# The first block of an fp32 Strassen MLP computed by plain products in four PSUM banks, with its queue neighbours moved

## The chip, the cores and the metric

The kernel runs on one core of one Trainium2 chip. The metric is the device time of one execution in microseconds (us). Engines are named as the profile names them: PE is TensorE (its weight loads are PEld), DVE is VectorE, ACT is ScalarE, POOL is GpSimd, SP is SyncE, whose queue SPq issues the DMA transfers.

## The reference

A retention attention (8 batches, 8 heads, 576 positions, head size 64) is followed by an MLP over its 4608 tokens. Cut to what matters:

```python
scores = np.matmul(q, k.transpose(0, 1, 3, 2)) / np.sqrt(64)
ret = scores * Dmat                     # causal, gamma[h] ** (distance)
x = np.matmul(ret, v)                   # -> [4608 tokens, 512]
h = x @ w_in                            # [512, 2048]
g = h * erf(softplus(h))
return g @ w_out                        # [2048, 512]
```

The weights arrive in double precision, as pairs of 32-bit words, and the kernel rounds them to fp32 on the chip.

## The kernel before

The MLP's products dominate. They run in blocks: 9 chunks of 512 tokens times 4 column groups of w_in. The block (g, c) needs x[g, c] and the weights of group g. Both matrix multiplications use Strassen's scheme, seven products of half-sized operands instead of eight. A product is four matmuls, which the trace shows as eight records of 1.9 us together. Attention is cut into stages (transposes, scores, outputs of 128-token pieces), and `attend` places them between the products of group 0. While the first block runs, attention has only just produced the first chunk, and the first group's weights are still being rounded.

The sums of x for Strassen's scheme, and the store of a chunk for use by later groups:

```python
xpool = tc.tile_pool(name="xpool", bufs=2)      # chunk 2 reuses the buffer of chunk 0

def store_x(c):
    nc.sync.dma_start(out=xd[c], in_=x_stored.pop(c))

def operands_x(g, c):                            # b11..b22: the quarters of the tile
    ...
    if g == 0:
        tt(t1, b12, b11, ALU.subtract)
        tt(t2, b22, t1, ALU.subtract)
        tt(b12, b22, b12, ALU.subtract)          # in place: b12 is overwritten
        tt(t4, b21, t2, ALU.subtract)
        x_stored[c] = t
```

One part of the weights is rounded in five steps; `round_weights(n)` takes n steps further. A group has eight parts, four of w_in (parts 1 to 4 below) and four of w_out:

```python
nc.scalar.activation(a_f, high_f, AF.Abs)                 # L220, ScalarE
nc.scalar.mul(out=r_f, in_=low, mul=2.0**-52)             # L221
yield
nc.vector.tensor_scalar(...)                              # L225, VectorE
yield
nc.vector.tensor_scalar(...)                              # L229
yield
nc.vector.scalar_tensor_tensor(...)                       # L233
yield
nc.vector.tensor_scalar(...)                              # L238
nc.gpsimd.tensor_tensor(out=r_f, in0=high_f, in1=r_f, op=ALU.mult)   # L239, GpSimd
nc.gpsimd.tensor_tensor(out=a_f, in0=a_f, in1=r_f, op=ALU.add)       # L240
load_weights()          # DMA of a later part; needs a free buffer of four
yield
```

The last step also issues the load of a later part, in SyncE's queue.

The order in which the first block was issued:

```python
    round_weights(5); attend(done[0] + 2); round_weights(5)
    operands_x(0, 0)
    attend(done[0] + 3)
    ...
    steps = firsts[0].first()               # products A11, A12
    next(steps); round_weights(5); attend(done[0] + 3); round_weights(9)
    next(steps); attend(done[0] + 1)
    run(firsts[0].middle(), (0, 2, 3))      # products S2, S3, S1
    run(firsts[0].last(), (3, 3))           # products S4, A22, then softplus
    store_x(0)
    firsts[0].erf()
    most[0] = stages_for(3 * TCH) - 1
    while done[0] < stages_for(2 * TCH):
        attend(done[0] + 1); round_weights(4)
    operands_x(0, 1); store_x(1)
    run(firsts[1].first(), (3, 3))
    firsts[0].multiply()
```

Of the kernel before, what the change touches and what calls it, by code (L numbers as in the profile page):

```python
# [11 lines left out]
FP32 = mybir.dt.float32  # L12
# [6 lines left out]
P = 128  # L19
# [26 lines left out]
def kernel(  # L46
# [10 lines left out]
    nc = tc.nc  # L57
# [3 lines left out]
    TH = TCH // 2  # L61
# [4 lines left out]
    GP = 2  # L66
    GW = GP * P
    n_g = FH // GW
    W = GP * TH
# [9 lines left out]
    gpool = ctx.enter_context(tc.tile_pool(name="gpool", bufs=2))  # L79
    opool = ctx.enter_context(tc.tile_pool(name="opool", bufs=2))  # L80
    ps_at = ctx.enter_context(tc.tile_pool(name="ps_at", bufs=4, space=PSUM))
    ps_a = ctx.enter_context(tc.tile_pool(name="ps_a", bufs=2, space=PSUM))
    ps_e = ctx.enter_context(tc.tile_pool(name="ps_e", bufs=1, space=PSUM))
# [5 lines left out]
    def tt(out, in0, in1, op):  # L89
        nc.vector.tensor_tensor(out=out, in0=in0, in1=in1, op=op)  # L90
# [58 lines left out]
    A11, S3, A12, A22, S1, S2, S4 = range(7)  # L149
    B11, T3, B21, B22, T1, T2, T4 = range(7)  # L150
    weights = {}
# [96 lines left out]
    def round_weights(n=1):  # L248
        for _ in range(n):
            next(round_step, None)  # L250
# [13 lines left out]
    x = {}  # L264
# [117 lines left out]
    done = [0]  # L382

    def stages_for(tokens):

        last = max(i for i, (b, s0, _) in enumerate(pieces) if b * S + s0 < tokens)
        return stages.index((outputs, last)) + 1

    def attend(upto):
        while done[0] < min(upto, len(stages)):  # L390
            of, i = stages[done[0]]
            of(i)
            done[0] += 1
# [6 lines left out]
    def store_x(c):  # L400
        nc.sync.dma_start(out=xd[c], in_=x_stored.pop(c))
# [3 lines left out]
    def operands_x(g, c):  # L405
        t = x[g, c]
        b11, b12, b21, b22 = (t[:, 2 * d : 2 * d + 2, h * TH : (h + 1) * TH] for d in range(2) for h in range(2))
        t1, t2, t4 = (t[:, n_dc + j, :].rearrange("p (d i) -> p d i", d=2) for j in range(3))
# [3 lines that stand above are left out]
            tt(b12, b22, b12, ALU.subtract)  # L412
            tt(t4, b21, t2, ALU.subtract)
            x_stored[c] = t
        x[g, c] = {A11: b11, A12: b21, S4: b22, A22: t4, S1: t1, S2: t2, S3: b12}

    class First:
# [42 lines left out]
        def last(self):  # L460
            self.product(S4, self.a, False)
            nc.scalar.copy(out=self.t2[:, 0], in_=self.a)  # L462
            yield
            self.product(A22, self.e, False)
            tt(self.t1[:, 1], self.e, self.t1[:, 1], ALU.add)
            self.s = gpool.tile([P, 2, 2, W], FP32, tag="s", name="s")
            for j, t in enumerate((self.t1, self.t2)):
                nc.scalar.activation(self.s[:, j], t, AF.Softplus)  # L468
            yield

        def erf(self):
            for j in range(2):
# [100 lines left out]
    firsts = [First(g, c) for g, c in order]  # L573
# [22 lines left out]
    round_weights(5)  # L596
    attend(done[0] + 2)
    round_weights(5)
    operands_x(0, 0)
    attend(done[0] + 3)  # L600


    most = [stages_for(2 * TCH) - 1]

    def run(steps, rounds=(), stages=1):

        for step, _ in enumerate(steps):
            attend(min(done[0] + stages, most[0]))
            round_weights(rounds[step] if step < len(rounds) else 0)

    steps = firsts[0].first()
    next(steps)
    round_weights(5)
    attend(done[0] + 3)
    round_weights(9)
    next(steps)
    attend(done[0] + 1)
    run(firsts[0].middle(), (0, 2, 3))
    run(firsts[0].last(), (3, 3))
    store_x(0)  # L620
    firsts[0].erf()
    most[0] = stages_for(3 * TCH) - 1
    while done[0] < stages_for(2 * TCH):
        attend(done[0] + 1)
        round_weights(4)
    operands_x(0, 1)
    store_x(1)
    run(firsts[1].first(), (3, 3))
    firsts[0].multiply()
    for b, nxt in zip(blocks[1:], blocks[2:] + [None]):  # L630
        n = order.index((b.g, b.c))
# [10 lines left out]
        elif n + 2 < n_s:  # L642
            f = firsts[n + 1]
# [53 lines left out]
```

## Time and profile before

| | before |
|---|---|
| time, median of 3 runs | 1086.6 us (1084.09 to 1086.61) |
| span of the profiled run | 1083.4 us, mean granted PE clock 0.99 |
| PE busy | 1053.2 us |
| PE idle between 37 and 103.4 us | 19.5 us |
| PE idle after 104 us | 2.1 us, then the end |

### The profile page before, as it was taken

To read this page: it belongs to the slowest core of one execution; us is meant where nothing else is said; L and a number is where in the kernel's file an instruction comes from. 1 tells how busy PE (TensorE), PEld (TensorE's weight loads), DVE (VectorE), ACT (ScalarE), POOL (GpSimd) and SP (SyncE) were. 2 spreads that over 40 slices of the span, in tenths; PEclk is the share of its full clock that TensorE was granted. 3 is DMA by queue.
4 is the path that set the end of the run, shared out by engine and by line. 5 is a ranking of instruction groups with operands and counts; after the bars stand their busy time and mean duration, and the time that the engine had idled before them with its cause. 6 is when DMAs were issued, how large, how long until landed. Compare 5 with 4: busy or idle time off the path is not lost.

```text
span 1083.4 us, 15779 instructions
## 1 busy us (share of the span) xinstructions
PE 1053.2 (97%) x6514; PEld 904.8 (84%) x6514; DVE 611.5 (56%) x942; ACT 395.2 (36%) x494; POOL 143.6 (13%) x142
## 2 busy tenths in 40 slices
PE   9596999999999999999999999999999999999997
PEld 7475888888888888888888888888888888888886
DVE  3856766576567664455565545565555444544544
ACT  2243323413414244433334444333344433333341
POOL 2523222131212300001001100100011000000000
PEclk9898999999999999999999999999999999999999
DMA  9968668686594252355555534545443333444432
GB/s 184 224 146 252 146 185 227 138 236 156 153 225 133 77 194 107 146 185 197 200 204 206 183 147 146 185 184 200 187 194 147 146 146 146 149 183 186 192 135 77
DMA packets 186488, 185.65 MB, mean 171 GB/s; under 512 B 148017, under 2 KB 160817, under 8 KB 178353
## 3 DMA queue, kind: packets, MB, share of 16 engines
q1 hardware_dynamic: 186272, 184.31, 54.5%
q8 instruction: 51, 0.84, 0.3%
q10 hardware_dynamic: 144, 0.33, 0.1%
q14 instruction: 21, 0.16, 0.0%
HBM read 130.36 MB, written 61.34 MB: 177 GB/s over the span
## 4 chain that ended last, share of the span: by engine, by line
PE 93%; DVE 3%; DMA 1%; POOL 1%; issue 1%; ACT 1%; SPq 0%; POOLq 0%; DVEq 0%
PE a L506 23%; PE a L426 23%; PE g L506 12%; PE g L426 11%; PE e L426 6%; PE e L506 6%; PE s L308 3%; PE o L320 3%; PE o L331 3%; PE kv L343 2%; PE pt_k L298 1%; DMA xd<-x 1%; PE idle L585 1%; DVE x L90 0%; DVE sT L90 0%
## 5 line engine op out<-in xcount | busy, mean ns | idle before, releaser
L426 PE MATMUL a<-x,wa 128*128 128x256 f32 x1152 | 277.7, 384 | 10.1 <-DVE x L90 6.1
L426 PEld LDWEIGHTS a<-x,wa 128*128 128x128 f32 x1152 | 217.8, 191 | 41.2 <-issue 6.3
L506 PE MATMUL a<-wb,s 128*128 128x256 f32 x864 | 205.8, 381 | 2.1 <-DVE o L90 2.1
L506 PEld LDWEIGHTS a<-wb,s 128*128 128x128 f32 x864 | 162.5, 190 | 25.9 <-DVE o L90 2.4
L90 DVE TENSOR_TENSOR t<-g,t 128x512 f32<-128x512 f32 x72 | 49.8, 692 | 163.2 <-ACT t L456 120.7
L426 PE MATMUL g<-x,wa 128*128 128x256 f32 x576 | 137.2, 381 | 0.0
L90 DVE TENSOR_TENSOR o<-a,o 128x512 f32<-128x512 f32 x108 | 74.3, 688 | 105.3 <-PE a L506 104.2
L426 PEld LDWEIGHTS g<-x,wa 128*128 128x128 f32 x576 | 108.2, 190 | 14.8
L239 POOL TENSOR_TENSOR wraw<-wraw 128x512 f32<-128x512 f32 x32 | 33.9, 1058 | 491.5 <-DVE wraw L238 195.3
L451 ACT COPY t<-a 128x512 f32<-128x512 f32 x36 | 21.1, 586 | 193.0 <-PE a L426 193.0
L90 DVE TENSOR_TENSOR t<-t,s 128x1024 f32<-128x1024 f32 x72 | 86.5, 1242 | 0.0
L468 ACT ACTIVATE s<-t 128x1024 f32<-128x1024 f32 x72 | 72.1, 1048 | 29.6 <-DVE t L90 29.6
L426 PE MATMUL e<-x,wa 128*128 128x256 f32 x288 | 71.8, 393 | 6.3 <-POOL wa L240 6.3
L462 ACT COPY t<-a 128x512 f32<-128x512 f32 x36 | 21.1, 586 | 146.7 <-PE a L426 146.7
L473 ACT ACTIVATE s<-s 128x1024 f32<-128x1024 f32 x72 | 72.1, 1049 | 0.4
L506 PE MATMUL g<-wb,t 128*128 128x256 f32 x288 | 68.6, 381 | 0.0
L506 PE MATMUL a<-wb,t 128*128 128x256 f32 x288 | 68.5, 381 | 0.0
L506 PE MATMUL e<-wb,t 128*128 128x256 f32 x288 | 68.5, 381 | 0.0
L506 PE MATMUL g<-wb,s 128*128 128x256 f32 x288 | 68.5, 380 | 0.0
L426 PEld LDWEIGHTS e<-x,wa 128*128 128x128 f32 x288 | 55.6, 196 | 14.9 <-POOL wa L240 6.9
L456 ACT COPY t<-a 128x512 f32<-128x512 f32 x36 | 21.1, 585 | 113.4 <-PE a L426 113.4
L90 DVE TENSOR_TENSOR sT<-s,cst 128x512 f32<-128x512 f32 (+1 forms) x80 | 47.0, 629 | 26.8 <-PE s L308 26.7
(64 smaller groups left out, 1243.1 us busy)
## 6 DMA issues: line engine op xcount, KB each, us to landing
x<-xd SPq DMA_DIRECT2D x27, 1792.0 KB, 10.7
od<-o SPq DMA_DIRECT2D x54, 512.0 KB, 3.8
o<-od SPq DMA_DIRECT2D x27, 1024.0 KB, 6.9
xd<-x SPq DMA_DIRECT2D x9, 1792.0 KB, 7.0
out_dram<-o SPq DMA_DIRECT2D x17, 512.0 KB, 2.8
raw_k<-in_k_dram SPq DMA_DIRECT2D x64, 128.0 KB, 4.7
raw_v<-in_v_dram SPq DMA_DIRECT2D x64, 128.0 KB, 3.8
wraw<-in_moe_w_in_dram SPq DMA_DIRECT2D x32, 256.0 KB, 4.7
```

The lines of the kernel that those rows point to most:

```text
L90: nc.vector.tensor_tensor(out=out, in0=in0, in1=in1, op=op)
L239: nc.gpsimd.tensor_tensor(out=r_f, in0=high_f, in1=r_f, op=ALU.mult)
L308: nc.tensor.matmul(ps[e][:n, p, :n], lhsT=t["kT"][r, p, :n], rhs=t["qT"][r, p, :n], start=True, stop=True)
L320: nc.tensor.matmul(o[e * D : (e + 1) * D, p, :n], lhsT=t["v"][:n, 2 * p + e, :], rhs=t["sT"][:n, e, p, :n], start=(p == 0), stop=(s0 == 0 ...
L331: nc.tensor.matmul(o[r, p, :n], lhsT=kept["state"][r, p, :], rhs=t["qT"][r, p, :n], start=False, stop=(p == NP - 1), skip_group_check=True,)
L343: nc.tensor.matmul(kv[e * D : (e + 1) * D, p, :], lhsT=t["k"][:n, 2 * p + e, :], rhs=t["v"][:n, 2 * p + e, :], start=(p == 0), stop=(p == ...
L426: nc.tensor.matmul(acc[:, j * TH : (j + 1) * TH], lhsT=weights["wa", self.g][:, a, d, j * P : (j + 1) * P], rhs=x[self.g, self.c][a][:, d, :],
L451: nc.scalar.copy(out=self.t1[:, 1], in_=self.a)
L456: nc.scalar.copy(out=self.t2[:, 1], in_=self.a)
L468: nc.scalar.activation(self.s[:, j], t, AF.Softplus)
L473: nc.scalar.activation(self.s[:, j], self.s[:, j], AF.Erf)
L506: nc.tensor.matmul(acc[:, tp, :], lhsT=left[:, j * TH + tp * P : j * TH + (tp + 1) * P], rhs=weights["wb", self.g][:, b, j, :], start=(sta ...
```

## The change

The intent is to let TensorE begin while weights are still being rounded. Strassen's second product, A12, already needs parts 3 and 4, and later ones need sums of x and sums of weights. Eight plain products need neither: the first four use only parts 1 and 2, and the last four add parts 3 and 4 in the same four PSUM banks. The four sums of x, which stood in VectorE's queue just before the block, move behind it, and the store of the chunk with them. Softplus and erf of the block, and the rounding of parts 3 and 4, take other places in their queues.

```diff
+        def plain(self):
+            acc = [ps_a.tile([P, W], FP32, tag="a", name=f"p{n}") for n in range(2)]
+            acc += [ps_e.tile([P, W], FP32, tag=n, name="p" + n) for n in "eg"]
             ...
+            for half, slots in enumerate(((A11, S3), (A12, A22))):
+                for n in range(4):
+                    tok, f = n // 2, n % 2
+                    for j in range(GP):
+                        for d in range(2):
+                            nc.tensor.matmul(acc[n][:, j * TH : (j + 1) * TH],
+                                lhsT=wa[:, slots[f], d, j * P : (j + 1) * P],
+                                rhs=t[:, 2 * half + d, tok * TH : (tok + 1) * TH], ...)
+                    if half == 1:
+                        nc.scalar.copy(out=(self.t2 if tok else self.t1)[:, f], in_=acc[n])
+                    yield
             ...
     round_weights(5)
-    operands_x(0, 0)
     attend(done[0] + 3)
+    round_weights(5)
             ...
-    steps = firsts[0].first()
-    next(steps)
-    round_weights(5)
-    attend(done[0] + 3)
-    round_weights(9)
-    next(steps)
-    attend(done[0] + 1)
-    run(firsts[0].middle(), (0, 2, 3))
-    run(firsts[0].last(), (3, 3))
+    for step, _ in enumerate(firsts[0].plain()):
+        attend(min(done[0] + 1, most[0]))
+        round_weights((0, 5, 0, 0, 2, 2, 2, 2)[step])
+    operands_x(0, 0)
     store_x(0)
-    firsts[0].erf()
+    round_weights(2)
     most[0] = stages_for(3 * TCH) - 1
     while done[0] < stages_for(2 * TCH):
         attend(done[0] + 1)
-        round_weights(4)
+        round_weights(3)
+    firsts[0].softplus()
     operands_x(0, 1)
     store_x(1)
-    run(firsts[1].first(), (3, 3))
+    for _ in firsts[1].first():
+        attend(done[0] + 1)
+        round_weights(3)
+    firsts[0].erf()
     firsts[0].multiply()
```

(Cuts are marked with dots; the matmul's arguments are joined to fewer lines. The lines that make softplus a method of its own are left out.)

More of the change, by code (lines that the diff above doesn't have):

```diff
@@ L465, in last, with softplus @@
             tt(self.t1[:, 1], self.e, self.t1[:, 1], ALU.add)
+            self.softplus()
+            yield
+        def plain(self):
+            acc = [ps_a.tile([P, W], FP32, tag="a", name=f"p{n}") for n in range(2)]
+            acc += [ps_e.tile([P, W], FP32, tag=n, name="p" + n) for n in "eg"]
+            self.t1, self.t2 = (gpool.tile([P, 2, W], FP32, tag=f"t{n}", name=f"t{n}") for n in (1, 2))
+            wa, t = weights["wa", self.g], x[self.g, self.c]
+            for half, slots in enumerate(((A11, S3), (A12, A22))):
[3 more added lines that the diff above has]
+                        for d in range(2):
+                            nc.tensor.matmul(
+                                acc[n][:, j * TH : (j + 1) * TH],
+                                lhsT=wa[:, slots[f], d, j * P : (j + 1) * P],
+                                rhs=t[:, 2 * half + d, tok * TH : (tok + 1) * TH],
+                                start=(half == j == d == 0),
+                                stop=(half == d == 1),
+                                skip_group_check=True,
+                            )
+                    if half == 1:
+                        nc.scalar.copy(out=(self.t2 if tok else self.t1)[:, f], in_=acc[n])
+                    yield
+        def softplus(self):
             self.s = gpool.tile([P, 2, 2, W], FP32, tag="s", name="s")
@@ L468, in last @@
                 nc.scalar.activation(self.s[:, j], t, AF.Softplus)
-            yield
         def erf(self):
```

## The prediction

> **What bounds the kernel now.** I read first the page's busy line, then its slices, then TensorE's list of waits in the first 200 us, then TensorE's instructions in order of time, then the other queues around each gap.
>
> ```profile
> PE 1053.2 (97%) x6514; PEld 904.8 (84%) x6514; DVE 611.5 (56%) x942; ACT 395.2 (36%) x494; POOL 143.6 (13%) x142
> ...
> PE   9596999999999999999999999999999999999997
> ...
> PEclk9898999999999999999999999999999999999999
> ```
>
> TensorE (PE) is the bound: 30 us of a span of 1083.4 us are not busy, and the only low slices are in the first 110 us (one slice is 27 us) and the last. From 104 us on, the waits list shows TensorE waiting 2.1 us in all, near the end. So a microsecond gained on TensorE before 104 us is gained at the end; nothing else is. The waits list of the first 200 us names the large ones (total, times, longest):
>
> ```profile
> PE e L426 <- POOL wa L240: 6.3, 2, 4.5
> PE a L426 <- DVE x L90: 6.1, 1, 6.1
> PE a L426 <- POOL wa L240: 4.0, 1, 4.0
> ```
>
> Line 426 is a Strassen product of the first matrix multiplication, L240 the last step of rounding one part of its weights. TensorE in order of time (start, length, instruction, count, idle before):
>
> ```profile
> 40.99 2.60 PE L426 MATMUL a<-x,wa 128*128 128x256 f32 x6 [3.97 <-POOL wa L240]
> ...
> 49.49 0.70 PE L426 MATMUL e<-x,wa 128*128 128x256 f32 x2 [1.80 <-POOL wa L240]
> 54.67 2.93 PE L426 MATMUL e<-x,wa 128*128 128x256 f32 x6 [4.48 <-POOL wa L240]
> ...
> 84.77 0.68 PE L308 MATMUL s<-qT,kT 64*64 64x64 f32 x16 [2.13 <-ACT kT L299]
> 85.39 3.47 PE L426 MATMUL e<-x,wa 128*128 128x256 f32 x8
> ...
> 95.58 3.75 PE L426 MATMUL a<-x,wa 128*128 128x256 f32 x8 [6.08 <-DVE x L90]
> ```
>
> With the small ones (0.29, 0.17, 0.62), idle time from 37 to 103.4 us is 19.5 us. A second loss is visible: eight records take 3.47 or 3.75 us after a gap, but 1.9 elsewhere. One-microsecond windows show a granted clock of 0.50 at 41.3-44.7, 51.6-58.4, 85.7-89.1 and 92.5-99.3 us. Busy time in them, times the missing clock, is about 1.7 + 1.9 + 1.7 + 1.9 = 7.2 us. So 26.7 us can be won here, 2.5% of the time, if every wait vanished.
>
> The 6.08 us at 95.58 end a longer story, seen in the queues of VectorE (DVE) and of DMA issue (SPq):
>
> ```profile
> 75.77 6.98 SPq L203 DMA_DIRECT2D wraw<-in_moe_w_in_dram  x4
> 82.80 0.59 SPq L401 DMA_DIRECT2D xd<-x  x1
> ```
>
> ```profile
> 92.17 0.42 DVE L90 TENSOR_TENSOR x<-o,cst 128x256 f32<-128x256 f32 x1 [8.01 <-DMA xd<-x]
> ```
>
> The store of the first chunk of x stands behind weight loads that wait for a raw buffer; it is issued at 82.8 and lands 9.3 us later; only then may VectorE write chunk 2 into that buffer, and only then come the sums of chunk 1, for which TensorE waits.
>
> **What the Trainium skill says.** "TensorE: Matmul & The Clock Gate", Part 1: the array's clock is halved after an idle window of about 3.4 us and restored after a busy one, and the window runs freely. The trace agrees: the half-clock stretches begin and end on a grid of 3.41 us (41.3, 44.7, 51.6, 58.4, 85.7, 89.1), and a gap of 2.13 us was enough where it left the window 62% idle. "SBUF — State Buffer", Who interferes with whom: a VectorE instruction with two SBUF inputs, or in a two-port mode, and a GpSimd instruction exclude each other; one with a single SBUF input does not. It agrees: the sums of x at 37.68 us took 5.26 us for four beside GpSimd, 2.61 at 94.03 without it, and L239 1.36 us instead of 1.04; the score masks, read from PSUM, took 1.28 for two either way.
>
> **The change, part by part.** Seven Strassen products of block 0 become eight plain ones: +1 product, 8 records, +1.9 us of TensorE. The four sums of x leave the VectorE queue at 37.7 us and come after the block; four combining additions (0.69 us each) vanish, off the path. A plain product of the first half needs only weight parts 1 and 2, so four of them, with the attention stages between, now cover the rounding of parts 3 and 4. I followed the built order of all queues by hand, with durations from this trace (product 1.9, outputs 2.66 with states, scores 1.09, a pair of transposes 0.88, an L225-L229-L233-L238 chain 0.46+0.45+0.70+0.43, L239+L240 2.4).
>
> Gap 1. Part 2 ends its VectorE chain at 37.77 as before. GpSimd no longer meets the x sums, so L239+L240 take 2.4 instead of 3.0: ready at 40.35, not 40.94. Idle 3.4 us, half clock again.
>
> Gap 2, at parts 3 and 4, closes. TensorE: first product to 44.0, transposes 45.1, product 47.0, attention outputs 48.65 (its kv matmuls release the VectorE queue), product 50.55, scores 51.65, product 53.55, transposes 54.45. Part 4: VectorE 48.65 + state and x 1.0 + chain 2.1 = 51.75, GpSimd to 54.25. The fifth product needs it at 54.8: no wait, with half a microsecond to spare. Before, this gap cost 1.80 + 4.48 and 1.9 of clock.
>
> The rest of the plain block runs to 66.7 and the next outputs to 69.35. **Here a new wait appears:** in VectorE's queue, between those outputs and the score mask of the next stage, now stand the tail of a rounding (0.45 + 0.70), all four sums of chunk 0 (2.6) and L238 (0.43). Mask ready at 69.35 + 1.05 + 4.2 + 0.6 = 75.2; TensorE has only scores and a short transpose pair left, to 71.0. Idle 4.2 us, then a half-clock window, -1.7. This does not depend on absolute times: about 5.8 us of VectorE against 1.65 of TensorE.
>
> The store follows the sums at 74.2-74.8 instead of 82.8 and now stands ahead of the blocked weight load. With its median of 7.0 us (5.7 to 9.3) it lands near 81.5; VectorE reaches the write at 80.7. Then the rounding tail, slowed by GpSimd, and two of chunk 1's sums end at about 86. TensorE, at half clock from 75.2 to 78.6, has done outputs, the first two products of block 1, scores and transposes by 84.8: idle 1.2 instead of 6.08, and a warm clock. The 2.13 us for kT at 84.77 vanishes: the erf calls and their table load no longer stand before that copy. After that I find 0.4 us for the next mask, and 1.5 for another (VectorE has a weight sum and a multiply before it): the outputs that started at 108.61 now start near 98.2 and end near 99.9 against 109.63.
>
> The sum: idle 3.4 + 4.2 + 1.2 + 0.4 + 1.5 = 10.7 us against 19.5; clock 3.4 against 7.2; one more product, 1.9. Saved 8.8 + 3.8 - 1.9 = 10.7 by this sum, 9.7 by the running times. Three rounding steps of the output weights move into the loop, where TensorE has no waits. I take 10 off the 1086.6 us median: 1076.5.
>
> **The rivals.** (a) VectorE becomes the early bound. For: gap 2's margin is 0.5 us and the mask wait is mine from the order alone; if GpSimd and VectorE exclude each other more than I counted, the fifth product waits 1-2 us and another half-clock window falls: gain 4-6, time 1081-1083. (b) The store still decides. For: it took 9.3 us once, under load; the DMA share in 30-50 us is above 1. Then the third product of block 1 waits 3-4 us and goes cold: 1080. Against: fewer loads are issued beside it now. (c) The change does what its author hoped, and the mask wait is short because VectorE got the sums done early: they depend on no TensorE wait except the block's end. Against: they stand behind the outputs in a strict queue. Then 5-6 us more: 1070. (d) The extra product merely replaces idle time and nothing moves: 1086. Against: waits of 10 us are cut by dependence, not by chance.
>
> **Range and chances.** The errors of some six waits, each about a microsecond, and of one or two clock windows of 1.7 us give 3-4 us; the runs of before spread by 2.5 us. 8 in 10: 1071 to 1082. Faster by over 2% needs 1064.9, 21.7 us of the 26.7: 2 in 100. Slower by over 2% would need a new loss of 30 us in a stretch of 70: 1 in 100.
>
> **What would show it.** Right: TensorE's list has no GpSimd wait above 1 us except one of 3-3.5 us near 40 us; one of about 4 us for a score mask near 71-75; the chunk-0 store issued near 74-75; two half-clock stretches instead of four. After 104 us no new waits. Wrong: a GpSimd wait near 54 us (step gap 2), a VectorE wait on the store above 3 us, no mask wait near 75, or a steady stretch after 110 us that is not the same length as before.

## More of the kernel before

PE is busy for 97% of the span, and the whole loss that can be won lies in the first tenth. The view of stretches shows where. Its columns are: the stretch, its length, then the busy time of PE, PEld, DVE, ACT and POOL with the number of instructions, the granted PE clock, the DMA share and GB/s. Two of its lines for the kernel before:

```profile
50.00:60.00 10.00, 5.52 (x21) 4.55 (x21) 6.04 (x8) 1.08 (x2) 3.94 (x4) 0.66 0.89 177
...
90.00:100.00 10.00, 4.42 (x25) 3.19 (x25) 5.96 (x12) 1.81 (x4) 1.72 (x2) 0.66 0.83 247
```

In each of these stretches of ten microseconds PE has work for about half, and the mean clock granted over the stretch is 0.66. No other engine is full in them (the DMA share is 0.89 and 0.83), so they look like waits on an order of things rather than on throughput.

## The result, and the profile after

| | before | after |
|---|---|---|
| time, median | 1085.86 us (4 runs, 1084.09 to 1086.61) | 1075.51 us (4 runs, 1075.12 to 1076.22) |
| ratio | | 0.9908, 95% interval 0.9891 to 0.9925 |
| span of the profiled run | 1083.4 us | 1074.0 us |
| PE idle in the stretch of the first two blocks | 19.5 us | 9.4 us (2.01 + 4.16 + 1.10 + 0.67 + 1.30 + 0.15) |

A ratio here is the mean time of one kernel's runs over the mean of the other's runs of the same rounds, so it is not quite the ratio of the medians. The change is 0.9% faster. The predicted 1076.5 us is 1 us off.

The page of the changed kernel, its slices of PE and of PE's clock (40 slices of 27 us):

```profile
PE   8888999999999999999999999999999999999997
...
PEclk9889999999999999999999999999999999999999
```

The deep slice that "before" had (a 5 in the second place) is gone, but the first four slices are still not full, and the clock is still below its full value in two of them.

The stretches of the changed kernel, with the columns explained above:

```profile
50.00:60.00 10.00, 10.00 (x97) 8.26 (x96) 4.02 (x8) 1.66 (x3) 3.96 (x4) 1.00 0.98 170
...
70.00:80.00 10.00, 5.84 (x57) 4.70 (x54) 8.29 (x15) 5.12 (x7) 4.22 (x5) 0.66 0.80 256
...
90.00:100.00 10.00, 8.55 (x63) 6.92 (x64) 9.97 (x13) 2.79 (x5) 6.63 (x4) 1.00 1.07 321
```

The hole at 50-60 us is closed, the one at 90-100 us nearly so, and a new one stands at 70-80 us. TensorE's largest waits in the first 200 us (line, what was waited for, total, times, longest):

```profile
PE o L320 <- ACT s L495: 4.2, 1, 4.2
PE o L320 <- DVE sT L90: 2.8, 5, 1.0
PE p L480 <- POOL wa L240: 2.0, 1, 2.0
...
PE a L426 <- DVE x L90: 1.1, 1, 1.1
```

Against the list of before, the GpSimd waits fell from 10.3 us to 2.0, the wait for the sums of x from 6.1 to 1.1, and a wait of 4.2 us in an attention output (L320) came in. TensorE in order of time in the changed kernel (start, length, instruction, count, idle before):

```profile
40.22 2.93 PE L480 MATMUL p<-x,wa 128*128 128x256 f32 x6 [2.01 <-POOL wa L240]
...
54.11 1.89 PE L480 MATMUL p<-x,wa 128*128 128x256 f32 x8
...
74.68 2.52 PE L320 MATMUL o<-sT,raw_v 128*64 128x128 f32 x16 [4.16 <-ACT s L495]
...
85.97 1.96 PE L426 MATMUL a<-x,wa 128*128 128x256 f32 x8 [1.10 <-DVE x L90]
...
98.82 0.40 PE L320 MATMUL o<-sT,raw_v 128*64 128x128 f32 x2 [1.30 <-issue]
...
100.85 1.99 PE L532 MATMUL e<-wb,t 128*128 128x256 f32 x8
```

The product at 54.11 is the fifth, the first that needs parts 3 and 4; it starts with no wait at all. The last line is the second product of the second matrix multiplication. In the kernel before, the same product stands here in TensorE's order of time:

```profile
110.22 1.99 PE L506 MATMUL e<-wb,t 128*128 128x256 f32 x8
```

So by this product the change is 110.22 - 100.85 = 9.37 us ahead. The spans differ by 1083.4 - 1074.0 = 9.4 us. All that was won was won before 101 us, and nothing was lost later. From there on, the list of either kernel has the same wait, of 2.1 us in total for an output tile.

What ended the new wait at 74.68 is seen in VectorE's order of time:

```profile
71.03 2.61 DVE L90 TENSOR_TENSOR x<-x 128x512 f32<-128x512 f32 x4
73.56 0.42 DVE L238 TENSOR_SCALAR wraw<-wb 128x512 uint32<-128x512 uint32 x1
73.90 1.28 DVE L90 TENSOR_TENSOR sT<-s,cst 128x512 f32<-128x512 f32 x2
...
80.09 0.42 DVE L90 TENSOR_TENSOR sums<-kv,state 128x256 f32<-128x256 f32 x1 [1.63 <-PE kv L343]
80.43 0.75 DVE L90 TENSOR_TENSOR x<-o,cst 128x256 f32<-128x256 f32 x2
...
83.70 4.42 DVE L90 TENSOR_TENSOR x<-x 128x512 f32<-128x512 f32 x4
```

The mask of the next scores (sT, third line) stands behind the four sums of chunk 0 (first line) and a rounding step. Its first instruction ends near 73.90 + 0.68 = 74.58, and TensorE goes on at 74.68. The waits list names a ScalarE activation as the releaser instead, one that ended at about 74.47. In two of the experiments below (sums behind the mask, sums deferred) the same matmul again follows its mask by 0.10 or 0.11 us while the list names another ScalarE instruction. And where the softplus is put elsewhere (experiment "activations back") the list names VectorE. So the mask is the releaser, and the name in the list is that of whichever other instruction finished about then.

The two lines of SyncE's queue that answer the held-up store of before:

```profile
73.67 0.34 SPq L401 DMA_DIRECT2D xd<-x  x1
76.68 1.67 SPq L203 DMA_DIRECT2D wraw<-in_moe_w_in_dram  x2
```

The store of chunk 0 is issued at 73.67 instead of 82.80, and now ahead of the weight loads. VectorE writes into the freed buffer at about 80.8 (the line at 80.43 above, its second instruction) with no wait, where before it had waited 8.01 us.

### The profile page after: what moved, and what is told of

It reads as the page before. It is cut to its first block, busy times and chain, and to the rows that moved or that the text cites. A ratio compares the mean times of both kernels' runs of the same rounds, so it can differ in the third digit from the quotient of the medians.

```text
span 1074.0 us, 15808 instructions
## 1 busy us (share of the span) xinstructions
PE 1053.1 (98%) x6522; PEld 905.2 (84%) x6522; DVE 610.3 (57%) x939; ACT 395.7 (37%) x494; POOL 146.3 (14%) x142
## 4 chain that ended last, share of the span: by engine, by line
PE 93%; DVE 3%; SPq 2%; issue 1%; DMA 1%; ACT 0%; POOL 0%; DVEq 0%; ACTq 0%
PE a L532 23%; PE a L426 22%; PE g L532 12%; PE g L426 11%; PE e L532 6%; PE e L426 6%; PE o L320 3%; PE s L308 3%; PE o L331 3%; SPq L131 2%; PE kv L343 2%; PE pt_k L298 1%; PE p L480 1%; DMA raw_v<-in_v_dram 1%; DVE x L90 1%
## 5 line engine op out<-in xcount | busy, mean ns | idle before, releaser
L426 PE MATMUL a<-x,wa 128*128 128x256 f32 x1120 | 266.8, 381 | 1.1 <-DVE x L90 1.1
L426 PEld LDWEIGHTS a<-x,wa 128*128 128x128 f32 x1120 | 210.5, 190 | 30.4 <-ACT kT L299 1.3
L90 DVE TENSOR_TENSOR o<-a,o 128x512 f32<-128x512 f32 x108 | 74.2, 687 | 105.6 <-PE a L532 104.2
L426 PE MATMUL g<-x,wa 128*128 128x256 f32 x560 | 133.2, 381 | 0.0
L426 PEld LDWEIGHTS g<-x,wa 128*128 128x128 f32 x560 | 105.3, 190 | 14.4
L451 ACT COPY t<-a 128x512 f32<-128x512 f32 x35 | 20.5, 586 | 184.9 <-PE a L426 184.9
L462 ACT COPY t<-a 128x512 f32<-128x512 f32 x35 | 20.5, 586 | 148.5 <-PE a L426 148.5
L426 PE MATMUL e<-x,wa 128*128 128x256 f32 x280 | 66.7, 381 | 0.0
L532 PEld LDWEIGHTS g<-wb,t 128*128 128x128 f32 x288 | 54.2, 190 | 7.6
L532 PEld LDWEIGHTS g<-wb,s 128*128 128x128 f32 x288 | 54.2, 190 | 7.5
## 6 DMA issues: line engine op xcount, KB each, us to landing
x<-xd SPq DMA_DIRECT2D x27, 1792.0 KB, 10.7
```

Of the source, the lines that this page charges most:

```text
L90: nc.vector.tensor_tensor(out=out, in0=in0, in1=in1, op=op)
L426: nc.tensor.matmul(acc[:, j * TH : (j + 1) * TH], lhsT=weights["wa", self.g][:, a, d, j * P : (j + 1) * P], rhs=x[self.g, self.c][a][:, d, :],
L451: nc.scalar.copy(out=self.t1[:, 1], in_=self.a)
L532: nc.tensor.matmul(acc[:, tp, :], lhsT=left[:, j * TH + tp * P : j * TH + (tp + 1) * P], rhs=weights["wb", self.g][:, b, j, :], start=(sta ...
```

## The experiments

All were timed in five rounds against the kernel before, each on the same chip as the runs of before that stand beside it, on three different chips. All outputs are right. The changed kernel was not run again beside them, so an experiment is set against it by the two ratios to before: a difference of 0.001 is 1.1 us. An interval is about 0.0015 wide to either side (0.0017 for the changed kernel), so differences under about 2.5 us, the two errors taken together, are not taken as shown by the times alone.

| run | edit of | median us (runs) | before us | ratio (95%) |
|---|---|---|---|---|
| changed kernel | | 1075.51 (4) | 1085.86 | 0.9908 (0.9891 to 0.9925) |
| sums behind the mask | changed | 1078.99 (5) | 1085.22 | 0.9943 (0.9930 to 0.9956) |
| sums deferred | changed | 1073.88 (4) | 1085.22 | 0.9898 (0.9883 to 0.9913) |
| store early | before | 1081.38 (5) | 1085.22 | 0.9964 (0.9952 to 0.9977) |
| activations back | changed | 1074.94 (4) | 1085.22 | 0.9908 (0.9895 to 0.9922) |
| third part late | changed | 1076.96 (6) | 1086.03 | 0.9914 (0.9899 to 0.9928) |
| part one first | changed | 1073.49 (4) | 1086.03 | 0.9878 (0.9862 to 0.9895) |
| deferred and part one first | changed | 1070.82 (4) | 1086.03 | 0.9856 (0.9840 to 0.9871) |
| store late | changed | 1080.26 (6) | 1086.03 | 0.9946 (0.9932 to 0.9960) |
| rounding in the gaps | changed | 1079.03 (5) | 1086.10 | 0.9943 (0.9929 to 0.9957) |
| all three | changed | 1068.76 (4) | 1086.10 | 0.9839 (0.9825 to 0.9852) |
| all three, store first | changed | 1063.99 (6) | 1085.44 | 0.9805 (0.9791 to 0.9819) |

My theory after the result: about 10 us of idle time are gone because the rounding gap at parts 3 and 4 closed and because the store left earlier; about 4 us came back as the mask wait. The rivals: the store's place is incidental; or the activations' move did part of it; or the mask wait is all that keeps the change from winning more.

### Store early, in the old kernel

This does one part of the change alone: in the kernel before, the store moves ahead of the block's middle. Its data has been ready since the sums.

```diff
     attend(done[0] + 1)
+    store_x(0)
     run(firsts[0].middle(), (0, 2, 3))
     run(firsts[0].last(), (3, 3))
-    store_x(0)
```

> The kernel before, with only the store of chunk 0 moved ahead of the blocked weight loads (Strassen's first block kept). My theory: the 8 us wait of VectorE for that store is gone, the third product of block 1 starts near 89.5-90.5 instead of 95.6, then a new wait of about 2 us for the transposed q eats some: 4 to 7 us faster than before, 1079 to 1082. So more than half of the gain is the store's place. Rival (the gain is the plain block's closing of the rounding gaps): under 2 us faster.

Measured: ratio 0.9964, 3.8 us faster than before, just under the expected range. SyncE's issue and TensorE's third product of block 1 in this run:

```profile
67.49 0.89 SPq L401 DMA_DIRECT2D xd<-x  x1
```

```profile
91.80 3.47 PE L426 MATMUL a<-x,wa 128*128 128x256 f32 x8 [2.61 <-DVE x L90]
```

The store left 15.3 us earlier, and the wait fell from 6.08 to 2.61 us, 3.5 us less. The product still ran at half clock (3.47 us), and the wait of 2.13 us for kT, which the erf calls cause, stayed. One moved line thus gives more than a third of what the whole change gives, not the more than half that was expected.

### Store late, in the changed kernel

The reverse: everything of the change stays, only the store goes back behind a weight load that has to wait for its buffer.

```diff
     operands_x(0, 0)
-    store_x(0)
     round_weights(2)
     most[0] = stages_for(3 * TCH) - 1
+    attend(done[0] + 1)
+    round_weights(3)
+    store_x(0)
```

> The changed kernel with only the store of chunk 0 moved back behind the blocked weight load. My theory: the store is issued near 78-79 instead of 73.7 and lands near 85-86, VectorE waits for it about 5 us, the third product of block 1 starts near 90-91 and at half clock: 5 to 7 us slower than the changed kernel, 1080 to 1083. Rival (the plain block alone carries the gain): within 1.5 us.

Measured: ratio 0.9946 against 0.9908, 4.1 us slower than the changed kernel, a little less than expected; the two intervals do not overlap. SyncE's queue and TensorE in this run:

```profile
76.22 1.21 SPq L203 DMA_DIRECT2D wraw<-in_moe_w_in_dram  x2
77.47 0.59 SPq L401 DMA_DIRECT2D xd<-x  x1
```

```profile
90.83 3.75 PE L426 MATMUL a<-x,wa 128*128 128x256 f32 x8 [6.35 <-DVE x L90]
```

The store is issued 3.8 us later, and the third product of block 1 starts 90.83 - 85.97 = 4.9 us later, at half clock again. Both directions agree: the store's place is worth about 4 us, and is not incidental.

### Sums behind the mask

Is the 4.2 us wait for the mask worth its length? Here the sums of chunk 0 and the store go behind the next attention stage.

```diff
-    operands_x(0, 0)
-    store_x(0)
     round_weights(2)
     most[0] = stages_for(3 * TCH) - 1
+    attend(done[0] + 1)
+    operands_x(0, 0)
+    store_x(0)
+    round_weights(3)
```

> The changed kernel, with the four sums of chunk 0 and its store moved behind the next score masks in VectorE's queue. My theory: the 4.2 us wait of the outputs near 75 us falls to 1-2 us, but the same VectorE work and the later store still stand before the sums of chunk 1, so the third product of block 1 starts at 85.5-86.5 as now (85.97), with a wait of 5-6 us and a half clock there. Time within 2 us of the changed kernel, 1074.5 to 1077.5. Rival 1 (the mask wait costs its own length plus the half clock): 5-6 us faster, 1070. Rival 2 (the trace's label is right and the outputs wait for ScalarE's softplus): the wait stays at about 4 us, time unchanged.

Measured: ratio 0.9943, 3.8 us slower than the changed kernel. My theory had no loss beyond 2 us and the third product of block 1 at 85.5 to 86.5; it started at 89.13. TensorE and VectorE:

```profile
71.50 2.52 PE L320 MATMUL o<-sT,raw_v 128*64 128x128 f32 x16 [1.75 <-ACT wraw L221]
...
89.13 3.35 PE L426 MATMUL a<-x,wa 128*128 128x256 f32 x8 [8.15 <-DVE x L90]
```

```profile
84.99 0.42 DVE L90 TENSOR_TENSOR x<-o,cst 128x256 f32<-128x256 f32 x1 [6.51 <-DMA xd<-x]
```

The mask wait fell from 4.16 to 1.75 us, and the wait for the sums of chunk 1 grew from 1.10 to 8.15. The store went out at 75.53, only 1.9 us later, but VectorE could write its buffer only at 84.99, so it took about 9.4 us to land; I had reckoned with 7. In the changed kernel the store took 6.1 us from issue to landing. In this run the third product hangs on the store, and the time before it is mostly waiting room. But the edit moved the store too, so it does not show what the mask wait alone costs. In the changed kernel the two are close: the store had landed at about 79.8, and VectorE wrote the buffer at about 80.8, after a wait of 1.63 us for the outputs behind the mask (the line at 80.09 above).

### Sums deferred

This takes the sums of chunk 0 out of the early phase altogether: only the four parts of x are stored, early, and the sums are made when chunk 0 is loaded for group 1.

```diff
-        nc.sync.dma_start(out=x[g, c], in_=xd[c])
+        n = n_dc if (g, c) == (1, 0) else n_dc + 3
+        nc.sync.dma_start(out=x[g, c][:, :n], in_=xd[c][:, :n])
...
-        if g == 0:
+        if g == 0 or (g, c) == (1, 0):
...
         round_weights((0, 5, 0, 0, 2, 2, 2, 2)[step])
+        if step == 4:
+            nc.sync.dma_start(out=xd[0][:, :n_dc], in_=x[0, 0][:, :n_dc])
-    operands_x(0, 0)
-    store_x(0)
...
-            if n + 2 < n_ch:
-                store_x(n + 2)
+            if n + 2 < n_ch or order[n + 2] == (1, 0):
+                store_x(order[n + 2][1])
```

> The changed kernel, with the sums of chunk 0 left out of the start altogether: four parts of x are stored early, and the sums are made in the second group of columns, after loading. My theory: the wait near 75 us falls to 1-2 us with no half clock, VectorE has 2.6 us less before chunk 1's sums and the store lands long before, so the third product of block 1 starts near 82 instead of 85.97, and the gain of about 4 us stays to the end: 1071 to 1072.5. Rival (VectorE is not what holds the start, but the store or GpSimd): under 1 us.

Measured: ratio 0.9898, about 1 us better than the changed kernel, within the error; expected was 4. The mask wait is 1.75 us, as it should be. But the third product of block 1 started at 84.06 after a wait of 2.69 us, because the four sums of chunk 1 took 5.41 us here, from 79.70, beside GpSimd's rounding; the same four took 4.42 us in the changed kernel, and four such sums alone 2.61. The earlier start of the sums ran into the rounding. That is the larger part of the miss. A smaller part was lost later, in group 1, where the four sums of chunk 0 now stand in VectorE's queue (at 396.82, for 2.61 us). By the product that the changed kernel starts at 100.85 this run is 3.0 us ahead (97.84), but its span is only 1.9 us shorter (1072.1), and TensorE has a wait in the second group that the changed kernel has not:

```profile
404.92 1.99 PE L427 MATMUL g<-x,wa 128*128 128x256 f32 x8 [0.84 <-DVE o L90]
```

The three later runs that defer the sums (deferred and part one first, all three, and store first) list the same wait of 0.8 us.

### Activations back

Softplus and erf go back right behind block 0.

```diff
+    firsts[0].softplus()
     operands_x(0, 0)
     store_x(0)
     round_weights(2)
+    firsts[0].erf()
...
-    firsts[0].softplus()
...
-    firsts[0].erf()
```

> The changed kernel with softplus and erf put back to directly behind block 0, as before. My theory: the table loads now run inside the wait that VectorE makes near 71-75 us, so they cost nothing: within 1 us of the changed kernel, 1075 to 1076.5. Rival (moving the activations gave the 2.1 us wait for the copy of k and its half clock, 3-4 us): 1079.

Measured: ratio 0.9908, the same as the changed kernel's. So the activations' move brings nothing that five rounds can see. The mask wait in this run's list of TensorE's waits, which ScalarE can no longer be named for:

```profile
PE o L320 <- DVE sT L90: 5.5, 4, 4.1
```

### Third part late

The early rounding of part 3 goes into the block's first step.

```diff
     attend(done[0] + 3)
-    round_weights(5)
...
-        round_weights((0, 5, 0, 0, 2, 2, 2, 2)[step])
+        round_weights((5, 5, 0, 0, 2, 2, 2, 2)[step])
```

> The changed kernel with the third weight part's rounding issued after the first product's stage, as before the change. My theory: VectorE's order stays and only ScalarE's first step moves behind the copies of q and k; the part is needed near 54 us and would be ready near 51: within 1 us of the changed kernel. Rival (the moved rounding is what closed the gap): a GpSimd wait of 2 us or more near 54 us, 2-4 us slower.

Measured: ratio 0.9914 against 0.9908, a difference inside the error. The trace shows a second GpSimd wait, of 1.4 us. So no gain from the early start of part 3 is shown; the times alone would not exclude 2 or 3 us.

### Part one first

What of the remaining gap at 40 us? In the changed kernel the first product needs parts 1 and 2. With the loop over d (which selects the part) outside the four banks, all half-products of part 1 come first.

```diff
-                for n in range(4):
-                    tok, f = n // 2, n % 2
-                    for j in range(GP):
-                        for d in range(2):
-                            nc.tensor.matmul(...)
-                    if half == 1:
-                        nc.scalar.copy(...)
-                    yield
+                for d in range(2):
+                    for tok in range(2):
+                        for f in range(2):
+                            n = 2 * tok + f
+                            for j in range(GP):
+                                nc.tensor.matmul(...)
+                            if half == d == 1:
+                                nc.scalar.copy(...)
+                        yield
```

> The changed kernel with the plain products regrouped by weight part: all four banks take part 1, then all take part 2, and so on. My theory: 3.8 us of TensorE work then stand between the first product and the first need of part 2, so the 2.0 us GpSimd wait near 40 us vanishes and with it a window or two of half clock (3.8 us lost there now): 3 to 5 us earlier in the plain block. The rest of the start is bound by VectorE's chain behind the attention outputs, which moves along with TensorE, so it stays to the end: 1071 to 1073. Rival (VectorE's queue is busy then anyway and takes it back): under 1.5 us.

Measured: 1073.49 us, ratio 0.9878, some 3.2 us better than the changed kernel by the ratios. The GpSimd wait is gone, and with it the half-clock stretch. In its place stands a wait of 1.96 us at 40.15 for a raw load of q: TensorE now arrives there before the data. The mask wait is 4.16 us, as before. This fits the expectation's reading, that the next wait behind takes part of the gain.

### Deferred and part one first

The two edits above together.

> Sums of chunk 0 deferred and products regrouped by weight part, together. My theory: the two gaps are apart, gains add: 7 to 9 us faster than the changed kernel, 1067 to 1069. Rival (one bound behind both): no better than the better of the two.

Measured: 1070.82 us, ratio 0.9856, 5.6 us below the changed kernel; expected were 7 to 9. The sum of the two single effects by their ratios is 0.0010 + 0.0030, and both together give 0.0052, so they do add up, but the third product of block 1 again waits for the sums of chunk 1, 4.23 us at 80.22 and at half clock. The step that I had mis-sized in "sums deferred" is the same here.

### Rounding in the gaps, all three, and store first

The last idea: the tail of a rounding stands before the mask in VectorE's queue, so the roundings should go into the block's own gaps and not into the loop after it.

```diff
-        round_weights((0, 5, 0, 0, 2, 2, 2, 2)[step])
+        round_weights((0, 5, 0, 9, 0, 5, 5, 0)[step])
...
-    round_weights(2)
     most[0] = stages_for(3 * TCH) - 1
     while done[0] < stages_for(2 * TCH):
         attend(done[0] + 1)
-        round_weights(3)
```

Alone, on the changed kernel:

> The changed kernel with only the rounding moved into VectorE's idle stretches, the sums of chunk 0 left where they are. My theory: the mask wait near 75 us falls from 4.2 to about 2.7, but the sums and the store (issued near 71-72, landing 79-81) still stand before the third product of block 1, which starts near 82-83 instead of 85.97: 2 to 4 us faster than the changed kernel, 1072 to 1074. Rival (amount of VectorE work does not matter): within 1 us.

Measured: 1079.03 us, ratio 0.9943, 3.8 us slower than the changed kernel: wrong in direction. SyncE's queue and VectorE tell why:

```profile
75.06 1.32 SPq L203 DMA_DIRECT2D wraw<-in_moe_w_in_dram  x2
76.48 0.54 SPq L401 DMA_DIRECT2D xd<-x  x1
```

```profile
86.39 0.42 DVE L90 TENSOR_TENSOR x<-o,cst 128x256 f32<-128x256 f32 x1 [4.85 <-DMA xd<-x]
```

The roundings took their loads with them, and so the two DMA instructions of a weight load came to stand ahead of the store again. The store's data were ready at about 74.5 (the sums of chunk 0 end at 70.37 + 4.17), and it was issued at 76.48. The sums of chunk 0 also ran beside GpSimd, 4.17 us instead of 2.61, so the mask wait stayed at 4.28.

Together with the two edits of the section before:

> The version with both changes (sums of chunk 0 deferred, products regrouped by weight part), with VectorE's work of rounding moved out of the full stretch from 68 us on into the stretches before, where VectorE sits idle waiting for attention outputs: the weight sums and part 5 behind the fourth step of the plain block, part 6 and 7 behind the sixth and seventh, nothing in the loop behind it. My theory (VectorE's sheer amount of work from 68 to 100 us is what bounds the start once the store and the mask are out of the way): the waits of 1.75 and 4.23 us and the half clock fall to about 1 us together; 4 to 6 us faster than that version, 1065 to 1067. Rival (the order of dependences, not the amount, or the DMA queue): within 1.5 us of 1070.8.

Measured: 1068.76 us, about 2 us above the expected range. The mask wait is down to 0.16 us. But here, too, the early store (issued at 69.53) stood behind a weight load that began to be issued at 68.10, VectorE waited 6.70 us for it, and TensorE 4.57:

```profile
68.10 1.39 SPq L203 DMA_DIRECT2D wraw<-in_moe_w_in_dram  x2
69.53 0.59 SPq L643 DMA_DIRECT2D xd<-x  x1
```

```profile
79.85 3.57 PE L427 MATMUL a<-x,wa 128*128 128x256 f32 x8 [4.57 <-DVE x L90]
```

If the store's place in the issue queue is the cause, then moving it alone must remove this wait:

```diff
-        if step == 4:
+        if step == 2:
             nc.sync.dma_start(out=xd[0][:, :n_dc], in_=x[0, 0][:, :n_dc])
```

> The last version but one (sums deferred, products regrouped, rounding in the gaps) with the early store of chunk 0 moved two steps up, ahead of the weight loads behind which it was issued at 69.5 us. My theory: it is issued near 61-62 and lands near 67-68, VectorE's 6.7 us wait for it vanishes, and with it TensorE's 4.6 us and the half clock of 1.7: 5 to 6.5 us faster than that version, 1062.5 to 1064.5. Rival (something else stands close behind the store: multiply, GpSimd, the loads of k and v): under 2 us.

Measured: 1063.99 us, ratio 0.9805. The time is in the expected range; by the two ratios it is 3.7 us faster than "all three", less than the 5 to 6.5 expected. It is the best version, 21.5 us below the kernel before by the medians and about 11 us below the change. Whether it passes 2% is not settled: the interval, 0.9791 to 0.9819, holds 0.98. TensorE in order of time:

```profile
74.87 1.89 PE L427 MATMUL a<-x,wa 128*128 128x256 f32 x8
```

The third product of block 1 has no wait. The store was issued at 63.05 and landed 6.8 us later, just before VectorE wrote the freed buffer, at about 70.6 to 71.3, without waiting. The granted clock is 1.00 in every stretch of ten microseconds from 30 to 110 us.

One further idea, a third buffer for x so that chunk 2 need not wait for the store at all, did not fit the core's memory and was only built. What it would give is open.

## Why the prediction was right

The sum of the terms, as predicted and as the trace of the changed kernel shows them. The clock's loss is counted here from start to start: how much longer a group of instructions took until the next one started than the same group does at full clock (the sixteen matmuls at 74.68 took 2.45 us until 77.13, where 1.02 is usual). That gives 2.0, 2.1, 1.8 and 1.9 us for the four stretches before, and 4.1 and 2.6 us for the two after.

| term | predicted, before to after | measured, before to after |
|---|---|---|
| idle of TensorE | 19.5 to 10.7 | 19.5 to 9.4 |
| loss by the clock | 7.2 to 3.4 | 7.8 to 6.7 |
| one more product | 1.9 | 1.9 |
| gain | 10.7 by the sum, 9.7 by running times | 10.1 + 1.1 - 1.9 = 9.3; 9.4 in the span |

The hit within 1 us is in part luck, since two errors offset each other: the idle time fell to 9.4 us, 1.3 lower than predicted, and the clock's loss hardly fell, to 6.7 us and not to 3.4. (The 7.2 and the 7.8 of before are the same stretches counted in two ways. By the prediction's way, half of the busy time at half clock, the changed kernel lost 8.2/2 + 4.9/2 = 6.6 us.)

**Gap 1, mis-sized in the clock.** The step "Idle 3.4 us, half clock again" held in its idle part for the code, but not in the trace of the changed kernel's profiled execution: part 2 was ready at 40.16, as predicted within 0.2, yet TensorE arrived late, since its clock had already been halved at 35.3 us and stayed so to 45.5. That made 2.0 us of idle time and 4.1 us of clock loss. In six of the experiments (activations back, third part late, store late, sums behind the mask, sums deferred, rounding in the gaps) the wait was 3.32 or 3.33 us. Their code is the same up to there, but for part 3's rounding in "third part late". In the first five the half clock lasted for one stretch of about 3.4 us, in the first of them a loss of 1.6 us; in the sixth it lasted for two, from 39.5 to 46.3 us. So the step's size is right for most of these executions, and the clock's part of it varies from one execution to the next. Wait and clock together came to 3.3 + 1.6 = 4.9 us in "activations back" and to 2.0 + 4.1 = 6.1 us here.

**Gap 2.** "No wait, with half a microsecond to spare": part 4 was ready at 54.07, and the fifth product began at 54.11 without a wait. The margin was 0.04 us and not 0.5, because TensorE ran 0.7 us earlier than I followed it. Two sums of the prediction were off here: its first product ends at 44.0, about a microsecond later than 40.35 and six matmuls at half clock (2.6 us) give, and its transposes end at 54.45, where it says that the fifth product needs part 4 at 54.8. Rival (a) had this margin as its point; it did not come to pass, and of the six experiments named above only "third part late" has a second GpSimd wait.

**The mask wait.** Predicted 4.2 us, measured 4.16, by the very four sums in VectorE's queue. This was the step that the trace of before did not show and that only the order of the queues gave. Rival (c), which denied it, fell. The clock loss after it was the mis-sized term: I had put one window of 1.7 us, and the half clock lasted from 72.8 to 79.6 us, two windows long, which cost 2.6.

**The store.** Predicted to be issued at 74.2 to 74.8, measured 73.67; predicted to land near 81.5, and landed 6.1 us after its issue, at about 79.8. Rival (b), that the store still decides, did not happen at this place of the store, but the experiments show how near it was: "sums behind the mask" delayed the store by 1.9 us, and the third product was 3.2 us late. That the store's order is a cause of the gain is shown both ways (3.8 us alone in the old kernel, 4.1 us lost when it was put back).

**The later waits.** The third product of block 1 was predicted at about 86 with an idle of 1.2 us, measured 85.97 and 1.10. Then 0.4 predicted and 0.67 measured; 1.5 predicted and 1.45 measured. The outputs predicted near 98.2 started at 98.82. No new wait came after 104 us. The wait of 2.13 us for kT went, as predicted, but the reason given for it was not needed. In "activations back" the erf calls stand before that copy again (erf from 72.87, the copy of kT at 75.04), and TensorE, held by the mask, comes to the scores that need it only at 80.16, without a wait.

**What the prediction did not say.** It did not weigh the parts of the change. By the experiments, the move of the activations gives nothing measurable, and for the early rounding of part 3 no gain is shown (0.7 us, inside the error). The gain comes from the store's earlier place, about 4 us, and, by the traces, from the closed gaps in rounding: GpSimd waits of 10.3 us became 2.0. What these gaps gave on their own, no run measured, since plain products without the whole of the store's move were only tried in "store late" (issued at 77.47, still 5.3 us sooner than before), which with 0.9946 is 5.9 us better than before and holds them, the activations' move and the mask wait at once.

## What to carry to other kernels

In these runs the issuing queue was a strict line, and so a transfer whose landing frees a buffer belongs ahead of loads that must themselves wait, and moving work that also issues loads moves those loads in that line. Before moving instructions off one engine's busy spot, write down what stands behind them in their new queue, and how long the bounding engine has other work; that alone gave the 4.2 us wait here within 0.1. And a removed wait pays only down to the next one behind it, so look for that one first: edits that singly gave 1 and 3 us, or lost 4, together gave 11 us once the store stood first and no large wait was left behind them.

## What the Trainium skill lacked or had wrong

- "TensorE: Matmul & The Clock Gate", Part 1, halves the clock after at least one idle window of some 3.4 us; the length of the window agrees (half clock from 35.3 to 45.5 us is three of them). But in the changed kernel the clock was halved at 35.3 us although TensorE had waited for only 1.04 us of the window before. The page tells further on of micro-idle times between groups of matmuls that make the clock oscillate, but gives no amount. Waiting time in the window alone does not decide: in the kernel before, the same wait of 1.04 us lay whole in one window (31.1 to 34.5 us) and the clock stayed full, and in "activations back" it stayed full after a window with 1.84 us of waiting (84.1 to 87.5 us). What decides, the runs do not tell.
- "SBUF — State Buffer", Who interferes with whom, has the rule that a VectorE instruction with two SBUF inputs contends with GpSimd, and the traces agree; it gives no duration for sums like these. Four fp32 sums of 128x512 took 2.61 us alone and 3.46 to 5.42 us where GpSimd instructions ran beside them.
- "DMA: Bandwidth & Descriptors", Queues, rings and completion order, tells that transfers need not complete in the order of their issue, but not that a transfer still to be issued is held up behind one that waits for its buffer in the same issuing queue. Before the change, weight loads occupied SyncE's queue for 6.98 us with the ready store behind them, and the store's place was worth about 4 us of the kernel's time.
- No page that I read warns that the releaser named for a wait can be an instruction that merely ended at about that time. Here a wait of 4.16 us was put down to a softplus of ScalarE, and the run with the softplus elsewhere still had it, at 4.1 us.
